# A linear-attention block feeding an erf-gated layer: where one projection piece stands between the chunk products and the end of the previous step's output

## The chip, the cores and the metric

The kernel runs on one core of one Trainium2 chip. The metric is device time in microseconds, the median of several runs. A profile is one execution of its own: it has a time of its own, and a span from its first to its last instruction.

## The reference

Two blocks in a row. The first is a recurrence (RWKV-6) over 768 tokens for 4 batches and 8 heads of 48 values; the second is a dense layer on its output.

```python
# r, k, v, w: (4, 8, 768, 48); u: (8, 48)
for t in range(S):
    cur = einsum('bhd,bhe->bhde', u * k[t], v[t])
    y[t] = einsum('bhd,bhde->bhe', r[t], state + cur)
    state = w[t][..., None] * state + einsum('bhd,bhe->bhde', k[t], v[t])
x = y.transpose(0, 2, 1, 3).reshape(3072, 384)
h = x @ w_in                        # (3072, 2048)
g = h * erf(softplus(h))
out = g @ w_out                     # (3072, 384)
```

All arithmetic is in fp32.

## The kernel before

The tokens are cut into chunks of 128 in two halves of 64. A step handles one chunk of two batches, so there are twelve steps, 0 to 11 (`n_steps`); steps five to eleven go through `attend_late`. Within a half, the products of r and k are made level by level over blocks of doubling width. In the late steps the small levels come from other engines, and TensorE makes levels five and six (`level_products`, L671: 48 rows against 48 or 32 columns). `take_level` (L681) puts the products of level five into the tile `own`, and `scale` (L364) multiplies r and k by the decays of the level, both on VectorE.

The output y of a step is gathered in a PSUM tile in these parts:

- `from_own(s, own, 1)`, the first half of the chunk's own part, 16 matmuls (32 records, L703);
- `fence()`, a small VectorE copy (L712) that reads y, and that the second half waits for;
- `from_own(s, own, 0)`, the second half, 32 records of L703;
- `through_state`, the part from the state, 64 records of L729, for the tiles `s` and `middle`. Behind it ScalarE copies y to `y3` (L737) and to `xT` (L758), and six small transfers on SP's queue (L764) complete `xT`, the input of the dense layer.

A late step finishes the y of the step before it: `before` is s - 1 when that is a late step too, and so is set in steps six to eleven. Between these parts stand pieces of the dense layer of earlier steps, so that TensorE always has something to do. They are named by letters in lists written out by hand, one for each place in the step (`USUAL`, and `LATE` for steps five and eleven); `run_late` carries them out:

- `P`, a piece of the projection of step s - 3 (`project_fast`, L1275: eight matmuls of 128 rows by 128 columns against 192, 16 records); the projection of two chunks takes seven pieces, the second into another PSUM tile, the fourth into what the first has left;
- `H`, a piece of the hidden layer of step s - 1 (`hidden`, L1153, 12 records), which reads `xT`;
- `s`, `ex`, `m`: softplus (L1109) and erf (L1113) on ScalarE, and the product with them on VectorE (L1118);
- `F`, the next stage of `prepare(s + 1)`: decays and small levels of the next step, on GpSimd and VectorE (its first GpSimd instruction, L486, refills the `own` tile of step s - 1).

The place "front" holds `s P` in all late steps. The order of instructions on each engine is the order in which the program issues them; all engines wait for each other by semaphores. The PSUM tiles `m` of the dense layer have two buffers; the tiles `own` and the inputs `in` have two as well, so the input of step s + 1 is loaded (`load_step`, L231) once `through_state` has read that of step s - 1.

Of the kernel before, what the change touches and what calls it, by code (L numbers as in the profile page):

```python
# [17 lines left out]
P = 128  # L18
# [73 lines left out]
def kernel(  # L92
# [71 lines left out]
    def products(shape, n=None):  # L164

        if n is None:
            n = turns["next"]
            turns["next"] = 1 - n
        names = "abc"[: len(shape) - 1]
        return banks[n][:].rearrange(  # L170
            f"p ({' '.join(names)}) -> p {' '.join(names)}", **dict(zip(names, shape[1:]))
        )
# [5 lines left out]
    def load_halves(dst, src):  # L178

        for i in range(2):  # L180
            nc.sync.dma_start(out=dst[:, i], in_=src[:, i])

    def load_w(s):
        ws[s] = ins.tile([P, JP, C], FP32, name="w")
        nc.sync.dma_start(out=ws[s][:], in_=rkw[s][:, 2])
# [34 lines left out]
    def load_v(s):  # L220

        vt = loaded[s][1]
        nc.sync.dma_start(out=vt[:], in_=v[s])

    def load_step(s):
        t = ins.tile([P, 2, JP, C], FP32, name="in")
        vt = ins.tile([P, NH, D], FP32, name="v")
        if s < DIRECT:
            load_halves(t, rkw[s])
        else:  # L230
            nc.sync.dma_start(out=t[:], in_=rkw[s][:, 0:2])  # L231
        if s == DIRECT:
            load_w(s)
        loaded[s] = t, vt
        if s > 3:
            load_v(s)
# [105 lines left out]
    def at(e, p):  # L342

        return rows(e ^ p & 1)
# [298 lines left out]
    def parts_of(s):  # L643

        c, i = divmod(s, SPC)
        in_t, vt = loaded[s]
        made, tots, tot = ready[s]
        ends = tot.rearrange("p (n h) -> p n h", h=NC)
        return c, in_t, vt, made, states[i][c % 2], states[i][1 - c % 2], ends

    def by_pair(t):

        return lambda x, n: t[:, x, n]
# [5 lines left out]
    def level_products(pp, rk, level, ns=range(NJ * NP)):  # L659

        half = 1 << (level - 1)
        m = HC - half if 1 < level <= MASKED else HC if level == 1 else half
        for n in ns:
            for s0 in range(0, C, HC):
                for e in range(NE):
                    right = rk(0, n)[rows(e), s0 : s0 + HC]
                    to = pp[s0 : s0 + m, e, n, :]
                    if level > 1:
                        right = rights(right, half)
                        to = to[:, : HC // 2].rearrange("p (b h) -> p b h", h=half)  # L670
                    nc.tensor.matmul(  # L671
                        to, lhsT=rk(1, n)[rows(e), s0 : s0 + m], rhs=right,
                        start=True,
                        stop=True,
                    )
# [18 lines left out]
    def from_own(s, own, swap):  # L694
        vt = loaded[s][1]
        for j in range(NJ):
            for q in range(0, NP, 2):
                for h in range(NC):
                    e = h ^ swap
                    for p in (q, q + 1):  # L700
                        n = j * NP + p
                        t = slice(h * HC, (h + 1) * HC)
                        nc.tensor.matmul(  # L703
                            y[at(e, p), e, p // 2, j, t],
                            lhsT=vt[t, n * NE + e, :], rhs=own[t, e * JP + n, :],
                            start=swap == 1 and not j and not q, stop=True,
                            skip_group_check=True,
                        )

    def fence():  # L710

        nc.vector.tensor_copy(  # L712
            out=seen[:].rearrange("p (e g t) -> p e g t", e=NE, g=NP),
            in_=y[:].rearrange("p e q j t -> p e (q j) t")[..., HC - 1 : HC + 1],
        )
# [96 lines left out]
    def attend_late(s, run):  # L812

        c, in_t, vt, own, S, S_next, ends = parts_of(s)
        RK = by_pair(in_t)
        before = s - 1 if s - 1 > DIRECT else None
        if before:
            from_own(before, ready[before][0], 1)
            fence()
        pp = products([P, NE, JP, HC], 0)  # L820
        level_products(pp, RK, LOG - 1)
        scale(s, LOG - 1)
        take_level(own, pp, LOG - 1)
        run("front", None)
        if before:
            from_own(before, ready[before][0], 0)
            through_state(before, xTs[before])
            if s + 1 < n_steps:
                load_step(s + 1)
        following = prepare(s + 1) if s + 1 < n_steps else iter(())  # L830
        next(following, None)
        nc.gpsimd.tensor_mul(faded[0][:], S[:], ends[:, :, 0:1].to_broadcast([P, JP, D]))
        next(following, None)
        run("near", None)
        next(following, None)
        kT = kTs[s]
        nc.vector.tensor_mul(
            kT[:].rearrange("p (e n) d -> p n e d", e=NE),
            kT[:].rearrange("p (e n) d -> p n e d", e=NE), spread[s][:],
        )  # L840
        run(0, following)

        pp = products([P, NE, JP, HC], 0)
        level_products(pp, RK, LOG)
        if s + 1 < n_steps:
            spread_blocks(s + 1, pp)
        take_level(own, pp, LOG)
        if s > DIRECT + 1:
            scale(s, LOG)
        run(1, following)  # L850
        if s == DIRECT + 1:
            scale(s, LOG)
        ps = products([P, NC, JP, HC], 0)
        ps = [[ps[:, h]] * NE for h in range(NC)]
        state_part(s, kT, ps)
        run(2, following)
        nc.vector.tensor_add(middle[both], faded[0][both], ps[0][0][both, :, :D])
        run(3, following)
        if s < n_steps - SPC:
            nc.gpsimd.tensor_mul(  # L860
                faded[1][:], middle[:], ends[:, :, 1:2].to_broadcast([P, JP, D])
            )
            nc.vector.tensor_add(S_next[both], faded[1][both], ps[1][0][both, :, :D])
        run(4, following)
# [243 lines left out]
    def softplus_chunk():  # L1108
        nc.scalar.activation(sp_room, chunks[0], AF.Softplus)  # L1109
# [6 lines left out]
    def multiply_chunk():  # L1116
        h, at = started.pop(0)
        nc.vector.tensor_mul(h, h, at)  # L1118
# [304 lines left out]
    def advance(count=None):  # L1423

        while later and count != 0:
            stage, last = later.pop(0)
            stage()
            count = count and count - 1
            if last and not count:
                break  # L1430
# [44 lines left out]
    def run_late(s, tokens, following=None):  # L1475

        for what in tokens.split():
            if what == "A":
                advance()
            elif what == "P":  # L1480
                piece(projs, s - 3)
            elif what == "H":
                piece(hids, s - 1)
            elif what == "F":
                next(following, None)
            elif what == "Q":
                piece(projs, s - 2)
            elif what == "J":
                next(turns["joint"])
            elif what == "w":  # L1490
                next(joining)
            elif what in "uvz":
                activate_pair(what)
            elif what == "T":
                turns["joint"] = hidden_of_two()
            elif what == "t":
                next(mixing_tokens)
            elif what == "f":
                turns.pop("fill")()
            elif what == "s":  # L1500
                softplus_chunk()
            elif what[0] == "e":
                erf_chunk(what[1])
            elif what == "m":
                multiply_chunk()
            elif what[0] == "k":
                to_lane(s - 2, what[1:3], what[3])
            else:
                blend(s - 2, *(int(n) for n in what[1:]))
                for name in {"S3": ("11", "22"), "S4": ("12",)}.get(what, ()):  # L1510
                    lanes.pop(name, None)
# [29 lines left out]
    with tc.manual_schedule(  # L1541
# [15 lines left out]
        for s in range(n_steps):  # L1557
# [44 lines left out]
            def run(n, following):  # L1602
                if n == 3 and s < n_steps - 2:
                    load_rows(s + 2)
                if n == 3 and s + 3 < n_steps:
                    load_w(s + 3)
                run_late(s, LATE.get(s, USUAL)[STAGES_LATE.index(n)], following)
# [12 lines left out]
        s = n_steps  # L1620
# [107 lines left out]
```

## Time and profile before

| | us |
|---|---|
| median of 3 runs | 575.22 (575.2 to 575.34) |
| the profiled execution, its own time | 574.36 |
| its span | 572.6 |
| TensorE matmuls busy | 564.2 |
| TensorE weight loads busy | 500.6 |
| projection pieces, L1275, in the chain that ended last | 33% of the span |
| hidden pieces, L1153, in that chain | 32% of the span |

The chain that ended last is followed back from the last instruction, at each step to what released it. TensorE has 89% of it, VectorE 5%, DMA 2%. The groups of instructions that the change touches (line, engine, shapes, count, then busy us and mean ns of one):

| line | what | count | busy us | mean ns |
|---|---|---|---|---|
| L703 | own part of y, 64 x 48 against 64 | 768 | 15.9 | 220 |
| L729 | state part of y, `middle`, 48 x 48 against 64 | 384 | 7.7 | 217 |
| L729 | state part of y, `s` | 320 | 6.4 | 217 |
| L671 | level five, 48 x 48 against 32 | 768 | 10.8 | 206 |
| L1275 | projection, `w_out_sb` by `h`, 128 x 128 against 192 | 320 | 56.2 | 329 |

Small matmuls of four array tiles run beside each other, so that their busy time in a timeline is much less than the sum of their durations.

### The profile page before, as it was taken

To read this page: it belongs to the slowest core of one execution; us is meant where nothing else is said; L and a number is where in the kernel's file an instruction comes from. 1 tells how busy PE (TensorE), PEld (TensorE's weight loads), DVE (VectorE), ACT (ScalarE), POOL (GpSimd) and SP (SyncE) were. 2 spreads that over 40 slices of the span, in tenths; PEclk is the share of its full clock that TensorE was granted. 3 is DMA by queue.
4 is the path that set the end of the run, shared out by engine and by line. 5 is a ranking of instruction groups with operands and counts; after the bars stand their busy time and mean duration, and the time that the engine had idled before them with its cause. 6 is when DMAs were issued, how large, how long until landed. Compare 5 with 4: busy or idle time off the path is not lost.

```text
span 572.6 us, 16719 instructions
## 1 busy us (share of the span) xinstructions
PE 564.2 (99%) x7320; PEld 500.6 (87%) x7320; DVE 452.7 (79%) x506; ACT 358.5 (63%) x495; POOL 246.8 (43%) x265
## 2 busy tenths in 40 slices
PE   8899999999999999999999999999999999999997
PEld 5688887578998998998998998898898899989997
DVE  8774886999899899799699599599599596477730
ACT  3658877645458858747756766766675771489500
POOL 4557380731885884384285185176075000000000
PEclk9999999999999999999999999999999999999999
DMA  7596671440426324245245236234232201000000
GB/s 256 199 297 269 224 224 43 187 158 10 148 64 188 104 63 163 38 158 168 35 145 176 40 121 198 41 112 166 47 112 84 47 9 35 2 2 1 27 29 27
DMA packets 54082, 63.24 MB, mean 110 GB/s; under 512 B 35161, under 2 KB 40569, under 8 KB 52985
## 3 DMA queue, kind: packets, MB, share of 16 engines
q1 hardware_dynamic: 53624, 61.98, 34.4%
q8 instruction: 57, 0.93, 0.7%
q10 hardware_dynamic: 384, 0.20, 0.1%
q14 instruction: 17, 0.13, 0.1%
HBM read 52.39 MB, written 8.69 MB: 107 GB/s over the span
## 4 chain that ended last, share of the span: by engine, by line
PE 89%; DVE 5%; DMA 2%; ACT 1%; POOL 1%; issue 1%; SPq 0%; DVEq 0%; ACTq 0%; POOLq 0%
PE m L1275 33%; PE m L1153 32%; PE c L1378 6%; PE pp L671 5%; PE m L1185 4%; PE y L703 2%; PE y L729 2%; PE pp L778 2%; DVE in L364 1%; DMA words<-in_moe_w_in 1%; PE pp L990 1%; PE pp L1063 1%; DMA u_sb<-in_u 1%; DVE h L1118 1%; POOL tot_sb L386 0%
## 5 line engine op out<-in xcount | busy, mean ns | idle before, releaser
L1153 PE MATMUL m<-xT,w_in_sb 128*128 128x256 f32 x960 | 214.9, 382 | 0.2 <-ACT h L1162 0.2
L1153 PEld LDWEIGHTS m<-xT,w_in_sb 128*128 128x128 f32 x960 | 179.9, 190 | 25.5 <-ACT h L1162 0.6
L364 DVE TENSOR_TENSOR in<-in,tot_sb 128x1024 f32<-128x1024 f32 (+1 forms) x55 | 77.4, 1408 | 5.9 <-PE pp L671 3.4
L1162 ACT COPY h<-m 128x512 f32<-128x512 f32 x80 | 46.3, 580 | 47.8 <-PE m L1153 47.5
L1275 PE MATMUL m<-mixed,h 128*128 128x192 f32 x320 | 56.7, 331 | 0.0
L1275 PE MATMUL m<-w_out_sb,h 128*128 128x192 f32 x320 | 56.2, 329 | 0.0
L1275 PEld LDWEIGHTS m<-mixed,h 128*128 128x128 f32 x320 | 51.8, 190 | 0.9
L1275 PEld LDWEIGHTS m<-w_out_sb,h 128*128 128x128 f32 x320 | 52.0, 190 | 0.5
L1275 PE MATMUL m<-w_out_sb,room 128*128 128x192 f32 x288 | 49.7, 326 | 0.0
L1275 PEld LDWEIGHTS m<-w_out_sb,room 128*128 128x128 f32 x288 | 47.3, 190 | 0.1
L1113 ACT ACT_TABLE_LOAD x28 | 35.9, 1283 | 10.5 <-DVE h L1118 8.4
L534 POOL TENSOR_TENSOR words<-words 128x384 f32<-128x384 f32 x28 | 39.7, 1448 | 0.0
L671 PEld LDWEIGHTS pp<-in 48*48 48x48 f32 (+4 forms) x2368 | 30.1, 120 | 10.9 <-issue 5.8
L493 POOL TENSOR_TENSOR words<-words,own 128x384 f32<-128x384 f32 x21 | 30.1, 1433 | 22.0 <-DVE words L524 13.0
L1109 ACT ACT_TABLE_LOAD x28 | 35.9, 1283 | 1.8 <-issue 1.3
L486 POOL TENSOR_TENSOR own<-rest 128x384 f32<-128x384 f32 x7 | 9.7, 1384 | 61.0 <-ACT o L1281 61.0
L671 PE MATMUL pp<-in 48*48 48x32 f32 (+4 forms) x2368 | 34.0, 206 | 0.3 <-DVE in L364 0.3
L534 POOL TENSOR_TENSOR rk<-words 128x384 f32<-128x384 f32 x28 | 33.4, 1225 | 0.0
L559 DVE TENSOR_REDUCE sums<-rk 128x16 f32<-128x768 f32 (+2 forms) x31 | 31.6, 1021 | 0.0
L438 POOL TENSOR_TENSOR tot_sb<-tot_sb 128x256 f32<-128x256 f32 (+4 forms) x50 | 29.9, 598 | 3.8
L1109 ACT ACTIVATE room<-h 128x1024 f32<-128x1024 f32 x28 | 29.6, 1057 | 0.3
L319 POOL TENSOR_TENSOR w_out_sb<-w_out_sb,rest 128x768 int32<-128x768 int32 x8 | 18.3, 2290 | 21.9 <-DVE w_out_sb L311 21.9
(214 smaller groups left out, 1008.7 us busy)
## 6 DMA issues: line engine op xcount, KB each, us to landing
in<-in_rkw SPq DMA_DIRECT2D x8, 1024.0 KB, 5.3
words<-in_moe_w_in SPq DMA_DIRECT2D x16, 384.0 KB, 6.3
words<-in_moe_w_out SPq DMA_DIRECT2D x16, 384.0 KB, 4.4
words<-in_rk_rows SPq DMA_DIRECT2D x8, 768.0 KB, 6.4
w<-in_rkw SPq DMA_DIRECT2D x11, 512.0 KB
v<-in_v SPq DMA_DIRECT2D x12, 384.0 KB, 5.7
out<-o SPq DMA_DIRECT2D x23, 192.0 KB, 3.0
in<-in_rkw SPq DMA_DIRECT2D x7, 512.0 KB, 5.9
```

What stands on the lines that cost most here:

```text
L364: nc.vector.tensor_mul(halves, halves, view(tots[level - 1], 0, [[1, n], [2, nb], [0, half]]))
L438: nc.gpsimd.tensor_mul(new, pair[:, :, 0], pair[:, :, 1])
L493: engine.tensor_mul(to, to, of[:, :, None, :].to_broadcast([P, NEAR // 2 // half, half, D]))
L534: engine.tensor_mul(to[:, i], r[:, half:], k[:, part * rows + i, None].to_broadcast([P, half, D]),)
L559: nc.vector.tensor_reduce(out=to, in_=of, axis=mybir.AxisListType.X, op=ALU.add)
L671: nc.tensor.matmul(to, lhsT=rk(1, n)[rows(e), s0 : s0 + m], rhs=right, start=True, stop=True,)
L1109: nc.scalar.activation(sp_room, chunks[0], AF.Softplus)
L1113: nc.scalar.activation(at, sp_room, AF.Erf)
L1153: nc.tensor.matmul(ps[:, ff, :], lhsT=w_in_sb[:, g * FG + f + ff, kk * P : (kk + 1) * P], rhs=xT[:, kk, :], start=kk == 0, stop=kk == KT - 1,)
L1162: nc.scalar.copy(h[:, f : f + FT, :], ps[:])
L1275: nc.tensor.matmul(to, lhsT=a[:, f], rhs=b[:, f], start=start and f == 0, stop=f == FG - 1, skip_group_check=True,)
L1378: nc.tensor.matmul(to[:, f], lhsT=turns["weights"][b][:, i * FT + f], rhs=turns["tokens"][a], start=a + b in STARTS and not f, stop=True, ...
```

## The change

In steps six to eleven, the list of the place "front" is split. Softplus stays where it was, directly behind `take_level`. The projection piece moves behind the second half of y from the chunk, the part through the state, and the load of the next step's input. Step five, which has no step before it of its kind, keeps the whole list.

```diff
         take_level(own, pp, LOG - 1)
-        run("front", None)
         if before:
+            run_late(s, "s")
             from_own(before, ready[before][0], 0)
             through_state(before, xTs[before])
             if s + 1 < n_steps:
                 load_step(s + 1)
+            run_late(s, "P")
+        else:
+            run("front", None)
         following = prepare(s + 1) if s + 1 < n_steps else iter(())
```

On TensorE this gives, for each of the six steps: level five (L671), L703, L729, piece one, piece two, where it was level five, piece one, L703, L729, piece two. On ScalarE the copy behind piece one (L1281) comes after the copies of y (L737, L758). On SP's queue and on VectorE and GpSimd the order of the instructions stays.

## The prediction

> **What bounds the kernel now.** I read the page first, then the busy time by step, then TensorE's and the vector engine's timelines across one step. The page says which engine to price by. Columns: busy us, share of the span, instructions.
>
> ```profile
> PE 564.2 (99%) x7320; PEld 500.6 (87%) x7320; DVE 452.7 (79%) x506; ACT 358.5 (63%) x495; POOL 246.8 (43%) x265
> ```
>
> A busy matmul row may still hide waits, so the stage itself is needed. This row is one late step, from its level-five products to those of the next step (window, length, then busy us of TensorE's matmuls, its weight loads, VectorE, ScalarE, GpSimd, granted clock, DMA share, GB/s).
>
> ```profile
> 366.07:410.37 44.30, 44.30 (x547) 40.60 (x540) 37.41 (x38) 29.24 (x38) 22.93 (x26) 1.00 0.35 105
> ```
>
> TensorE has work in flight for all of the 44.30 us at full clock. The three steps ahead of it are 44.30 us each too. Asked for TensorE's waits between 277 and 490 us, the trace names none. So the end moves only by what TensorE itself spends, or by a new wait on it. Its timeline around the edit (start, busy us, what):
>
> ```profile
> 366.07 0.89 PE L671 MATMUL pp<-in 48*48 48x32 f32 x64
> 366.89 2.87 PE L1275 MATMUL m<-w_out_sb,h 128*128 128x192 f32 x16
> 369.69 0.67 PE L703 MATMUL y<-own,v 64*48 64x64 f32 x32
> 370.17 0.63 PE L729 MATMUL y<-in,s 48*48 48x64 f32 x32
> 370.62 0.63 PE L729 MATMUL y<-in,middle 48*48 48x64 f32 x32
> 371.18 2.87 PE L1275 MATMUL m<-mixed,h 128*128 128x192 f32 x16
> 373.88 2.76 PE L1275 MATMUL m<-w_out_sb,room 128*128 128x192 f32 x16
> 376.48 2.76 PE L1275 MATMUL m<-mixed,room 128*128 128x192 f32 x16
> ```
>
> Read start to start, since the busy times overlap. A projection piece costs 2.60 between two others (373.88 to 376.48), 2.70 behind small matmuls (371.18 to 373.88), and 2.80 with small ones on both sides (366.89 to 369.69). A piece set between two small groups thus pays 0.20 that one in a row of pieces does not, and small groups pay as well where a piece follows: 0.45 for the 32 matmuls from 370.17 to 370.62, but 0.56 for the next 32, ahead of a piece. The step is now small, piece, small, piece; the change makes it small, small, piece, piece.
>
> **The change part by part.** No instruction is added or removed; in each of steps six to eleven the first projection piece (L1275, 16 records) moves behind 32 records of L703 and 64 of L729.
>
> TensorE, start to start, before: 0.82 (L671), 2.80 (piece one), 0.48 (L703), 0.45 and 0.56 (L729), 2.70 (piece two), 2.60 (piece three), in all 10.41. After:
> - L671 no longer ends on a piece. Its 64 records are busy for 0.89, of which the last takes 0.21 (median of that line), so the last starts at 0.68; the next small one follows one spacing later (0.68 over 15 intervals of four is 0.045, of which the four's own starts use some), say 0.71. Gain 0.11, the same as the 0.56 less 0.45 of L729.
> - L703 no longer follows a piece: 0.45 as L729 has, not 0.48. Gain 0.03.
> - L729 still ends on a piece: 0.45 and 0.56 as before.
> - Piece one now follows small ones and is followed by a piece: 2.70, not 2.80. Piece two lies between pieces: 2.60, not 2.70. Gain 0.20.
>
> That is 0.34 a step, 10.07 for 10.41, and for six steps 2.04 us. All of it lies on the engine that has no slack, so it counts in full.
>
> The one seam that the step of before does not contain is L671 followed by L703. Two rows bound it. Level one in step one is followed by state products (64 rows by 48 columns, the shape of L703), and level six by L791; weight loads show it best.
>
> ```profile
> 31.06 1.00 PEld L671 LDWEIGHTS pp<-in 48*62 48x62 f32 x64 [0.33 <-DVE own L1034]
> 31.97 0.81 PEld L778 LDWEIGHTS pp<-v,kT 64*48 64x48 f32 x32
> ...
> 381.77 0.65 PEld L671 LDWEIGHTS pp<-in 48*32 48x32 f32 x64 [0.23 <-issue]
> 382.46 0.20 PEld L791 LDWEIGHTS pp<-ident,over_blocks 48*64 48x64 f32 x4
> ```
>
> In the first pair L778's first load starts at 31.97, before L671's loads end (32.06): no seam. In the second there is a hole of 0.04 (382.42 to 382.46), as ahead of a piece, and the seam costs the 0.11 that a piece costs. I take the first pair: level five's weights are 48 columns wide, like L703's, and those of level six 32. If the second held, L671 keeps 0.82 and L703 its 0.48: gain 0.20 a step, 1.2 us in all.
>
> [...]
>
> [...]
>
> **Waits.** L703 waits on VectorE for the fence (L712, which reads y), and now does so 2.80 sooner.
>
> ```profile
> 366.32 0.17 DVE L712 COPY seen<-y 128x16 f32<-128x16 f32 x1 [3.50 <-PE y L703]
> 367.03 1.23 DVE L364 TENSOR_TENSOR in<-in,tot_sb 128x1024 f32<-128x1024 f32 x1 [0.54 <-PE pp L671]
> 368.18 0.71 DVE L681 COPY_PREDICATED own<-mask_sb,pp 128x512 f32<-128x512 int32 x1
> ```
>
> The fence ends at 366.49 (VectorE idle for 3.50 before it); L703 would start at 366.07 + 0.71 = 366.78, its load some 0.05 ahead. With a hand-over from VectorE to a waiting TensorE of about 0.05 (0.07 is seen the other way, L703's end at 366.25 to the fence at 366.32) the slack is about 0.2. Level five's products are its cover; without them each late 0.1 us costs 0.6 over six steps. In step six VectorE has been idle for 1.86 and in the others for 3.5, so the cover holds. Cost nothing.
>
> Edits that cost nothing, with their cover. ScalarE: softplus (367.59 to 368.65) ends before the state products would (about 368.2 plus 0.2), so the copies of y run near 368.7 instead of 371.31; the piece's copy to o (L1281, 0.32) falls behind them, when the piece ends near 371.1, and then the load for erf (372.53 now) at about 371.4. Nothing on ScalarE is later. Piece four, which writes over what L1281 reads, comes two pieces (5.2) behind piece one. SP: the six xT transfers and the next step's input come 2.7 earlier, and xT is wanted at 388.97 by L1153. GpSimd: L486, which refills the own tile that L703 has read, starts at 370.52 now and may start near 367.9; VectorE's L518 waits 0.43 for what follows from it. VectorE is earlier, not later, for TensorE's later needs (the kT product, the sums that free m). In the last part TensorE's wait for the scalar copy at 540.63 (0.3) moves along.
>
> So 2.04 off 574.36, the profiled execution's own time (span 572.6), is 572.3; the median of the runs shown is 575.22, 0.86 above, and the same saving gives 573.2.
>
> **Rivals.**
> 1. The seam drains (the 382.46 pair). For it: a real row of the same line. Against: other tile width. 575.22 - 1.2 = 574.0.
> [...]
> 3. Slower: L703's wait covers more of VectorE than the fence. In the trace of before L703 starts at 369.69, behind the end of both L364 (368.26) and L681 (368.89), so the trace can't exclude that it waits for take_level. If so TensorE stands from 366.78 to about 368.94, 2.16 a step, less 0.34, times six: 575.22 + 10.9 = 586. Against: in the built program the count waited for is that of the fence, one below that of the scale. It turns a gain to a loss from a wait of 0.34 a step on.
> 4. The time is given back: a later wait on TensorE appears, most likely where H's second m buffer waits for VectorE's sum (ends 389.25, wanted at 388.97 + 1.31 = 390.28, slack 1.0). The shift of 0.34 leaves 0.7. It would give 575.2.
>
> **How the numbers follow.** Forecast 0.80; rival one 0.06; two 0.05; three 0.04; four 0.05. About 0.2% (1.15 us) is what a measurement can tell from no change. Faster: forecast and rival one, 0.86. Same: two and four, 0.10. Slower: three, 0.04. Forecast alone, with 0.30 to 0.38 a step: 572.9 to 573.4. The range adds the seam's other bound (574.0) and 0.1 for the spread of the runs: 572.8 to 574.1.
>
> **What would show it.** In the trace after: a step of 43.96 instead of 44.30; L671 to L703 0.71 start to start, no idle ahead of L703's loads; piece one 2.70 and piece two 2.60; L712 still 0.25 behind L671's start. Wrong would be an idle time of TensorE with VectorE as its releaser at L703, a hole of 0.04 or more in the loads at that seam, or steps still 44.30 long.

## The result, and the profile after

The kernel after takes 577.97 us (median of 16 runs, 575.58 to 583.04), the kernel before 574.68 beside it (16 runs, 572.63 to 579.56). The ratio is 1.0058, with an interval of 1.0033 to 1.0084: slower by some 3.3 us. The forecast of 573.2 was wrong in sign, and its range (to 574.1) does not reach the result. Of the 16 runs after, six have a mean granted clock of 0.994 to 0.997 and take 578.28 to 583.04, ten have 0.999 or 1.0 and take 575.58 to 578.45. The profiled execution took 576.16 (span 574.3), where that of before took 574.36 (572.6).

The page still has TensorE's matmuls (PE) busy for nearly the whole span; before, they were busy for 564.2 us, 99%:

```profile
PE 563.3 (98%) x7320; PEld 500.8 (87%) x7320; DVE 454.5 (79%) x506; ACT 359.0 (63%) x495; POOL 246.4 (43%) x265
```

The steps say more. These are steps seven to eleven of the kernel after, from the level-five products of one step to those of the next (step eleven to the start of its L778), with the columns of the prediction's row:

```profile
276.01:319.98 43.97, 43.97 (x547) 40.53 (x540) 37.53 (x38) 29.25 (x38) 23.45 (x26) 1.00 0.40 118
319.98:364.23 44.25, 44.23 (x546) 40.50 (x540) 37.53 (x38) 29.32 (x38) 23.45 (x26) 1.00 0.40 117
364.23:409.62 45.39, 44.28 (x547) 40.69 (x540) 37.06 (x38) 29.51 (x38) 22.57 (x26) 1.00 0.36 103
409.62:455.31 45.69, 44.27 (x516) 40.69 (x509) 36.95 (x37) 29.48 (x38) 18.31 (x16) 1.00 0.27 76
455.31:478.21 22.90, 21.75 (x350) 21.03 (x340) 19.24 (x27) 13.41 (x19) 0.00 (x0) 1.00 0.05 15
```

Step seven is 43.97 long, and so is step six: the 43.96 that was forecast, 0.33 less than the 44.30 of every step before. Step eight has 44.25, nine 45.39, ten 45.69, and the part of step eleven 22.90 where it had 21.79. The six differences are -0.33, -0.33, -0.05, +1.09, +1.39 and +1.11, in all +2.88. (The unchanged program ahead of step six took 1.13 less in this one execution, so the spans differ by only 1.7.) So two steps gained what was said, one hardly gained and three lost, although the edit is the same in all six. TensorE's timeline of step seven:

```profile
276.01 0.89 PE L671 MATMUL pp<-in 48*48 48x32 f32 x64
276.72 0.64 PE L703 MATMUL y<-own,v 64*48 64x64 f32 x32
277.18 0.63 PE L729 MATMUL y<-in,s 48*48 48x64 f32 x32
277.63 0.63 PE L729 MATMUL y<-in,middle 48*48 48x64 f32 x32
278.19 2.87 PE L1278 MATMUL m<-w_out_sb,h 128*128 128x192 f32 x16
280.89 2.76 PE L1278 MATMUL m<-mixed,h 128*128 128x192 f32 x16
```

L1278 is L1275 of before. And of step nine:

```profile
364.23 0.89 PE L671 MATMUL pp<-in 48*48 48x32 f32 x64
364.94 0.64 PE L703 MATMUL y<-own,v 64*48 64x64 f32 x32
365.40 0.63 PE L729 MATMUL y<-in,s 48*48 48x64 f32 x32
365.85 0.50 PE L729 MATMUL y<-in,middle 48*48 48x64 f32 x18
367.46 0.43 PE L729 MATMUL y<-in,middle 48*48 48x64 f32 x14 [1.11 <-issue]
```

The first three rows stand as in step seven. Then TensorE stops in the middle of 32 matmuls of one line, between the 18th and the 19th, for 1.11 us, and no semaphore ends that: "issue" means that it waited for nothing that the profile shows. In step ten the stop lies between two products with `s` (412.83, 1.42), in step eleven behind the fourth with `middle` (458.35, 1.15). Among TensorE's waits in the whole trace after, these three come first; that of before has none at this line:

```profile
PE y L729 <- issue: 3.7, 3, 1.4
```

(us in total, times, the longest). The chain that ended last holds the three stops as pieces called "issue", 1.11, 1.42 and 1.15 us long.

**Counting the instructions.** Take all of TensorE's records in order of time: matmuls, weight loads, and 90 others, nearly all of them for semaphores. The number of records ahead of each of the three stops leaves the same remainder, 193, on division by 256; such a place in the count is called a border here. (Without the 90 others the remainders differ.) A small stop in step eight (0.34 from one start to the next, inside the moved piece, whose row lasts 3.15 there) does so too. The page's DMA section has a queue of instructions whose size fits TensorE's, the same in both kernels (packets, MB, share):

```profile
q8 instruction: 57, 0.93, 0.7%
```

0.93 MB over 57 packets are 16,384 bytes each, and some 14,700 records of TensorE over 57 are 256 and a bit: one packet brings 256 instructions. (The run below with 1,536 more instructions, six blocks, has 63 packets there.) Cut to the window from 364.4 to 367.6, the DMA view of the kernel after holds one packet and nothing else:

```profile
GB/s 0 0 0 0 0 0 0 205 0 0 0 0 0 0 0 0 0 0 0 0 0 0 0 0 0 0 0 0 0 0 0 0 0 0 0 0 0 0 0 0
...
q8 instruction: 1, 0.02, 2.0%
```

The slices are 0.08 us wide, and the eighth holds the packet's start: 365.03. 2.0% of 16 engines' 3.2 us is 1.02 us. So the border of 256 was passed at 364.40 (behind the 18th matmul of L671), the packet started 0.63 later, was in at 366.03, and TensorE went on 1.43 after that, at 367.46: 3.06 us for a block of 256. The rows of step seven show how fast the small matmuls pass such a block when they are not held: the 46 others of L671 in 0.54, L703 in 0.46, 32 of L729 in 0.45 and 18 in 0.25, about 1.7 us. The theory (F) is that TensorE runs out of instructions.

Before, the piece between level five and L703 lay inside this block: border at 366.24, packet from 367.12 to 368.48, next border at 370.62, that is 4.38 us, and 2.14 from the packet's end to the border, against the 1.43 of the stop in step nine. The piece, 2.80 us, has 32 of the 256 instructions; without it the block reaches 16 products (0.23) further into L729. 4.38 less 2.80, less the 0.14 of the two seams, and 0.23 more are 1.7 again; 3.06 less 1.7 is the stop of step nine (1.32 from start to start).

In steps six and seven the border falls at the end of L671 or behind it (233.05, 276.69), so that the next 256 instructions reach into the projection pieces: 6.6 us for the block of step seven, and no stop. Where a border falls inside L671 or just ahead of it (320.40, 364.40, 409.52, 455.32), the row that follows waited for its rest: 0.34 from one start to the next in step eight, then 1.11, 1.42 and 1.15. In step eight it falls latest, behind about 42 of the 64, so that the next border lies ten records into the moved piece, and the stop is small.

### The profile page after: what moved, and what is told of

The parts are those of the page before. It is cut to its first block, busy times and chain, and to the rows that moved or that the text cites. A ratio compares the mean times of both kernels' runs of the same rounds, so it can differ in the third digit from the quotient of the medians.

```text
span 574.3 us, 16725 instructions
## 1 busy us (share of the span) xinstructions
PE 563.3 (98%) x7320; PEld 500.8 (87%) x7320; DVE 454.5 (79%) x506; ACT 359.0 (63%) x495; POOL 246.4 (43%) x265
## 4 chain that ended last, share of the span: by engine, by line
PE 82%; DVE 8%; issue 4%; POOL 2%; DMA 2%; ACT 1%; SPq 0%; DVEq 0%; POOLq 0%; ACTq 0%
PE m L1278 33%; PE m L1156 29%; PE c L1381 6%; PE pp L671 5%; DVE in L364 2%; PE m L1188 2%; PE y L703 2%; PE y L729 2%; PE pp L778 1%; DMA words<-in_moe_w_in 1%; PE pp L993 1%; DMA u_sb<-in_u 1%; DVE own L681 1%; POOL w_out_sb L1219 1%; DVE h L1121 1%
## 5 line engine op out<-in xcount | busy, mean ns | idle before, releaser
L1278 PE MATMUL m<-w_out_sb,h 128*128 128x192 f32 x320 | 56.4, 330 | 0.0
L1278 PE MATMUL m<-mixed,h 128*128 128x192 f32 x320 | 56.1, 329 | 0.0
L1278 PEld LDWEIGHTS m<-w_out_sb,h 128*128 128x128 f32 x320 | 51.9, 190 | 1.0 <-issue 0.3
L1278 PEld LDWEIGHTS m<-mixed,h 128*128 128x128 f32 x320 | 52.1, 190 | 0.4
L1278 PE MATMUL m<-w_out_sb,room 128*128 128x192 f32 x288 | 49.7, 326 | 0.0
L1278 PEld LDWEIGHTS m<-w_out_sb,room 128*128 128x128 f32 x288 | 47.3, 190 | 0.1
L671 PEld LDWEIGHTS pp<-in 48*48 48x48 f32 (+4 forms) x2368 | 30.1, 120 | 11.2 <-issue 6.0
L671 PE MATMUL pp<-in 48*48 48x32 f32 (+4 forms) x2368 | 34.0, 206 | 0.4 <-DVE in L364 0.4
```

Of the source, the lines that this page charges most:

```text
L671: nc.tensor.matmul(to, lhsT=rk(1, n)[rows(e), s0 : s0 + m], rhs=right, start=True, stop=True,)
L1278: nc.tensor.matmul(to, lhsT=a[:, f], rhs=b[:, f], start=start and f == 0, stop=f == FG - 1, skip_group_check=True,)
```

## The experiments

The rivals to theory F were that the load of the next step's input, which now starts ahead of the piece, gets in the way (L), and that the stop is tied to the order or the place of the instructions rather than to their count.

**The load put back behind the piece.** The kernel after, with

```diff
             through_state(before, xTs[before])
+            run_late(s, "P")
             if s + 1 < n_steps:
                 load_step(s + 1)
-            run_late(s, "P")
```

> The change, with the load of the next step's input put back behind the projection piece (all transfers of the load then start where they did before). Theory F (TensorE runs out of instructions: they come in blocks of 256, and the small matmuls pass a block in under 2 us, faster than the next block comes): nothing changes on TensorE, its holes in the state products of steps 9, 10 and 11 stay at 1.1 to 1.4 us each, at the same instructions, and the time stays about 3 us above before (577 to 578.5). Rival L (the 1 MB load, started earlier, gets in the way of what TensorE reads or fetches): the holes are gone, steps 43.97 long, 2 us below before.

Measured: 578.92, ratio 1.007 (1.0044 to 1.0097). Steps six to ten 43.97, 43.97, 44.60, 45.68, 45.65. The stops are at the same instructions:

```profile
371.82 0.43 PE L729 MATMUL y<-in,middle 48*48 48x64 f32 x14 [1.40 <-issue]
```

Again the 19th product with `middle` of step nine. With the load back in its old place the stops are no shorter, so L falls. (The start of this program is that of the kernel after, and yet its trace has one more stop there, of 1.92 at 20.24 and also at remainder 193, behind a packet that started 3.4 after its border: one trace of a kernel doesn't show all that the next may have.)

**128 more instructions in step five,** in the kernel after and in the kernel before: the products of level five are made twice there, which gives the same values.

```diff
         level_products(pp, RK, LOG - 1)
+        if s == DIRECT + 1:
+            level_products(pp, RK, LOG - 1)
```

> The change, with the level-five products of step five made twice, which puts 128 more instructions (64 matmul records, 64 weight loads) on TensorE ahead of step six and some 0.75 us. Nothing else moves. Theory F: the borders of the 256-instruction blocks shift by half a block against the steps, so the holes leave steps 9, 10, 11 and appear in steps 6, 7 and 8, some 1.3 to 1.6 us each; steps 9, 10, 11 become 43.9 to 44.0 long. Rivals L and W (a wait on data that is late in the late steps): the holes stay in 9, 10, 11.

Measured: 578.14, ratio 1.0056 (1.0029 to 1.0083). The steps six, seven and nine of it:

```profile
234.35:279.74 45.39, 44.21 (x547) 40.63 (x540) 37.07 (x38) 29.51 (x38) 22.57 (x26) 1.00 0.38 114
279.74:325.36 45.62, 44.19 (x547) 40.60 (x540) 37.52 (x38) 29.51 (x38) 22.45 (x26) 1.00 0.38 114
...
369.33:413.30 43.97, 43.97 (x547) 40.53 (x540) 37.53 (x38) 29.25 (x38) 23.43 (x26) 1.00 0.37 106
```

The loss has changed places: steps six and seven have it now, nine to eleven are free. Nothing in those steps was edited against the kernel after; only the count of instructions ahead of them is another (and the start of step six, 2.3 us later). Both stops are at remainder 193 again. One part missed: step eight was to have a stop and has none. There the border lay at 324.99, in L703 ahead of L671; TensorE was still in the slow hidden pieces when the next packet started, at 322.28, 2.7 before the border. The block then passed in 1.62 us without a stop, which is the free pace of the row of small matmuls.

> The kernel before with the same doubled products in step five. Theory F: the piece between the small groups keeps every block above 4.3 us, so no hole appears at any phase of the blocks: steps six to ten stay 44.30 long, and the time is before plus 0.75. If holes of over 0.3 us appeared here, the phase would matter without the change as well, and the change alone would not be what makes them.

Measured: 574.89, ratio 0.9997 (0.9976 to 1.0018), all late steps 44.30 and no stop. This shift of the phase (where the borders fall in a step) does nothing by itself while the piece is in its old place.

**The change in steps six and seven alone.**

```diff
         if before:
-            run_late(s, "s")
+            late = s in (6, 7)
+            run_late(s, "s" if late else "s P")
 ...
-            run_late(s, "P")
+            if late:
+                run_late(s, "P")
```

> The change in steps six and seven alone; steps eight to eleven as before. Theory F: no block border pair falls inside the small matmuls of these two steps, so both are 43.97 long and all others 44.30, no hole anywhere, the time 0.7 below before (ratio 0.9988). Rivals L and W, by which any step that has the change can get a hole: 43.97 or a hole of about 1 us, not the same in each run.

Measured: 573.56, ratio 0.998 (0.996 to 1.0). Steps 43.97, 43.97, 44.30, 44.30, 44.29, and TensorE has no wait of any kind in the late steps.

**The piece between L703 and L729,** in all six steps. L703 is as early as in the kernel after, and the row of small matmuls is cut behind it.

```diff
             run_late(s, "s")
             from_own(before, ready[before][0], 0)
+            run_late(s, "P")
             through_state(before, xTs[before])
             if s + 1 < n_steps:
                 load_step(s + 1)
-            run_late(s, "P")
```

> Half of the change in steps six to eleven: the second half of y from the chunk directly behind level five, then the projection piece, then the part through the state. As many seams between small matmuls and pieces as before, so nothing is saved; the longest run of small matmuls is 256 instructions (first half, level five, second half) instead of 384. Theory F: a block of 256 takes at least the 2.8 us of the piece, or is asked for before the run begins, so there is no hole, every step is 44.30 long, and the time is that of before. Rival W (the state products stop for data of their own): the holes stay in steps 9 to 11.

Measured: 573.49, ratio 0.9982 (0.9962 to 1.0001), all steps 44.31, no stop. So it is not the early L703 that costs; the piece covers the supply in this place as in its old one. There is also no gain in the steps, because this order has as many seams as that of before.

**Only small matmuls for six blocks.** The kernel before, with the level-five products of step five made thirteen times, 1,536 more instructions.

```diff
+        if s == DIRECT + 1:
+            for _ in range(12):
+                level_products(pp, RK, LOG - 1)
```

> The kernel before with the level-five products of step five made thirteen times: 1536 more instructions in a row, which are six whole blocks, so that the phase of later steps stays. It prices the supply by itself. The array alone would take 12 times 0.71, 8.5 us. Theory F: each block of 256 waits for its own transfer, 3.0 to 3.8 us from border to border, so six blocks take 18 to 23 us, with a hole at every border and all later steps at 44.30. Rivals L and W: 8.5 us, no hole.

Measured: 600.78, one run; step five 69.82 instead of 43.12. Its timeline:

```profile
193.38 2.79 PE L671 MATMUL pp<-in 48*48 48x32 f32 x128 [1.82 <-issue]
197.38 2.79 PE L671 MATMUL pp<-in 48*48 48x32 f32 x128 [1.21 <-issue]
203.30 2.78 PE L671 MATMUL pp<-in 48*48 48x32 f32 x128 [3.14 <-issue]
```

Each row is 128 matmuls with their 128 weight loads, one block, and a stop lies on either side of each. From border to border it takes 3.45 to 4.00 us, once 5.92, where the packet started only at 201.09, 3.7 behind the border, beside other transfers of up to 441 GB/s. That supply is a limit is shown; the sum was missed, 26.7 where 18 to 23 were expected (the bare matmuls were to cost 8.5). One reason is that packet, the other stands in the busy time by stretch, with the granted clock in the third column from the end:

```profile
193.38:197.38 4.00, 2.79 (x128) 2.65 (x128) 0.00 (x0) 2.34 (x2) 0.14 (x1) 0.50 0.24 51
215.00:222.00 7.00, 7.00 (x47) 6.94 (x44) 6.46 (x9) 1.28 (x2) 1.64 (x1) 0.62 0.01 2
```

From 193.01, within the first of the stops, the clock is granted at half: a row of 128 takes 2.79, where the 142 ahead of that stop, at the full clock, took 1.78. The work behind the rows pays for it too, with 0.62 over 7 us.

**Half of the piece ahead, half behind.** The kernel before; piece one is cut behind its fourth product, and the second half moves behind `through_state`.

```diff
             from_own(before, ready[before][0], 0)
             through_state(before, xTs[before])
             if s + 1 < n_steps:
                 load_step(s + 1)
+            run_late(s, "P")
```

```diff
-        product(m0[:, lo], a11, b11, True)
+        for f in range(FG):
+            nc.tensor.matmul(
+                m0[:, lo], lhsT=a11[:, f], rhs=b11[:, f], start=f == 0, stop=f == FG - 1,
+                ...
+            )
+            if f == FG // 2 - 1 and 3 <= s <= 8:
+                yield
```

> The kernel before with the first projection piece of steps six to eleven cut in two: four matmuls stay ahead of the second half of y (1.5 us of cover instead of 2.8), four go behind the state products. Seams cost what they did (5.50 for pieces one and two), so steps without a hole are 44.30. Theory F: the block that holds the run takes about 3.2 us unhindered in steps 9 to 11, and the next block comes 3.0 to 3.8 us after the border: holes of 0 to 0.6 us there, none in steps 6 and 7. A cover that only mattered by being there or not would give no hole at all.

Measured: 574.52, ratio 1.0026 (1.0003 to 1.0048). Steps eight to ten:

```profile
321.35:365.64 44.29, 44.29 (x546) 40.59 (x540) 38.13 (x38) 29.35 (x38) 23.28 (x26) 1.00 0.40 117
365.64:410.32 44.68, 44.60 (x547) 40.76 (x540) 38.14 (x38) 29.36 (x38) 23.27 (x26) 1.00 0.36 104
410.32:454.69 44.37, 44.37 (x516) 40.67 (x508) 37.66 (x37) 29.36 (x38) 19.13 (x16) 1.00 0.28 78
```

Half a piece is 1.50 us of cover. The blocks of steps nine to eleven last 3.54, 3.18 and 3.15, with a stop of 0.29 in step nine and next to nothing in ten and eleven. The length of the cover counted here: 1.7 of free pace and 1.5 of piece come to 3.2, about what the supply took in these steps of the kernel after (3.0 to 3.3).

**Steps eight to eleven alone, with the phase set at the program's start:** 33 small matmuls take the place of one warm-up matmul, 128 instructions more by count.

```diff
-        stay_warm(6)
+        stay_warm(5)
+        pass_by(33)
```

> Made from theory F: the change in steps eight to eleven alone, with the blocks shifted by half a block from the start (one of the six warm-up matmuls at the start gives way to 33 small ones, 128 instructions more). Steps 6 and 7 keep the old order, since after the shift their run would hold a border pair. Theory F: steps 8 to 11 are 43.97 long, 6 and 7 44.30, no hole, the time 1.3 below before (573.0) if the start is as long as before. Rivals: holes in steps 9 to 11 as in the full change, 4 us above that.

Measured: 578.21, ratio 1.008 (1.005 to 1.0111). The late steps came as expected, 44.30, 44.30, 43.97, 43.97, 43.96, without a stop. The start did not: level five of step six begins at 237.69 instead of 233.17. The early part has small matmuls too, and the new phase put borders among them while the weights were being loaded:

```profile
22.78 0.48 PE L1004 MATMUL pp<-s,ident 128*128 128x384 f32 x1 [2.16 <-issue]
39.97 0.35 PE L671 MATMUL pp<-in 48*60 48x32 f32 x10 [1.18 <-issue]
```

The packets of these two blocks started 3.0 and 3.8 us after their borders (17.41 and 33.76). The two stops, 3.3 in all, fit theory F: a shift can be paid for wherever else the count decides. How much of the 4.5 is the shift's is not shown, since in the first 50 us of the traces of before and after six packets start 3.0 to 4.0 behind their borders, and the unshifted start had a stop too in the run with the load behind the piece.

**All six steps, with the phase set behind step seven.** The kernel after, with the level-six products of step seven made twice: 128 more instructions in a group of small ones far from the edit. Beside it the version with steps six and seven alone was timed again.

```diff
         level_products(pp, RK, LOG)
+        if s == DIRECT + 3:
+            level_products(pp, RK, LOG)
```

> The kernel after, with the products of level six of step seven made twice: 128 more small TensorE instructions in a group that already has small ones, far from the edit, so no new seam. Theory F (TensorE runs out of instructions in the long row of small matmuls where a border of 256 falls just ahead of it): steps six and seven keep their phase and are free of holes, steps eight to eleven take the phase of the kernel with 128 more in step five, which is free in these steps. Steps 43.97, 43.97 plus the doubled group's 0.65 to 0.7, then 43.97, 43.97, 43.97, 43.96 and a last part of about 21.5. Over the six steps about 1.3 less than before; time 572.9 to 573.6 where before has 574.3, ratio 0.997 to 0.9985. If the loss came from the order itself (transfers, later waits, whatever is not tied to the count of instructions), steps eight to eleven stay at 44.25 to 45.7 and the kernel is slower than before by 0.7% as the kernel after is.

Measured: 572.66, ratio 0.9973 (0.9955 to 0.9992), before 574.58. Steps seven to ten:

```profile
276.08:320.58 44.50, 44.50 (x610) 41.06 (x604) 37.55 (x38) 29.38 (x38) 23.44 (x26) 1.00 0.41 117
320.58:364.55 43.97, 43.97 (x547) 40.53 (x540) 37.52 (x38) 29.24 (x38) 23.40 (x26) 1.00 0.40 118
364.55:408.52 43.97, 43.97 (x547) 40.53 (x540) 37.54 (x38) 29.23 (x38) 23.43 (x26) 1.00 0.37 106
408.52:452.48 43.96, 43.96 (x516) 40.52 (x508) 37.08 (x37) 29.24 (x38) 19.29 (x16) 1.00 0.28 79
```

The 64 useless matmuls cost 0.53 in step seven, and all six steps have the 0.33: 220.37 from step six to step eleven instead of 221.49, and 0.34 less in step eleven. It adds work to the kernel after and is faster than that of before.

> The change in steps six and seven alone, timed again beside the other, since its interval just reached 1. Steps 43.97, 43.97, then 44.30; no holes in late steps; 0.66 less than before in the late steps, ratio 0.998 to 0.9995.

Measured: 573.56, ratio 0.9983 (0.9966 to 1.0), steps 43.97, 43.97, 44.30, 44.30, 44.29 and no late stop. The gain of 0.66 that its trace shows lies at the edge of what this measurement can tell: the piece between L703 and L729 had 0.9982 too, with no step shorter than before. It is the steps in the traces that carry the gain, here and with all six steps.

## Why the prediction was wrong, point by point

- **The seams** were right. L671 to L703 takes 0.71 (forecast 0.71), L703 to L729 0.46 (0.45), piece one 2.70, piece two 2.60, the step 43.97 (43.96). Rival one, the drain, did not come.
- **The load of L703** is not held. In step nine its first load starts at 364.91, while the last of L671's loads end at 365.01 and its last product, 0.21 long, has just started. The chance of rival two, 0.05 for 574.4, was that of a load held until that product is out, which no run shows.
- **The fence** costs nothing, as said: TensorE has no wait on VectorE at L703 in any step. Rival three falls, and with it the mechanism on which the whole chance of "slower" stood.
- **No later wait** took the gain back: where no instruction is missing, as in the last version, the steps are 43.97 long (44.50 with the added products) and TensorE waits for nothing in them. Rival four falls.
- **The step that failed** is "edits that cost nothing, with their cover". The moved piece was priced as 16 records with two seams, and as cover for the fence. It was also the cover under which the next 256 instructions came in: 2.80 us in a block that without it passes in 1.7 and takes 3.0 to 3.3 to supply in these steps. The statement that no instruction is added or removed was true, and beside the point: what counted here is how many instructions follow each other without slow work among them. Now level five, L703 and L729, with the 64 instructions of L703 ahead of them, are 384 in a row.
- **The trace of before could have told it.** The prediction rests on the waits between 277 and 490 us, where TensorE has none. In the list for the whole span, which was on hand, TensorE's second wait is one without a releaser, in the weight part of the start:

```profile
PE pp L671 <- issue: 0.8, 1, 0.8
```

  It is a stop in the middle of 32 equal matmuls at 27.88, also at remainder 193; its packet ran from 25.62 to 26.51, and TensorE went on 1.38 later. In steps nine to eleven of the same trace the packets start 0.88, 0.94 and 0.89 behind their borders and take 1.36, 1.24 and 0.95. With 1.38 taken for each as the time to go on, the three blocks take 10.4 to supply, and without the piece they pass in three times 1.7: 5.3 lost, less six times 0.34, is slower by some 3.3. That sum is made with hindsight; the traces have 2.9, with other packet times and a little lost in step eight, the medians 3.3.
- **The chance** of slower, 0.04, was that of one mechanism, the fence. Cover was counted on the engines and queues that the edit touches by name; the engine's own supply of instructions was not among them.

Left open: why some packets start late (3.0 to 4.0 us behind the border for three in the first 50 us of the trace of before and three in that of after, between which and their borders 273 to 408 GB/s were moved; not isolated), and how much of the spread of the runs comes from them, since each kernel has one trace. What lowered the clock to 0.994 to 0.997 in six of the runs after was not shown either.

## What to carry to other kernels

Before slow work is moved out of a row of small instructions, count the instructions that will then follow each other, and compare the time in which they pass with the time in which the engine's instruction queue brings them; here 256 small ones pass in 1.6 to 1.7 us and come in 3.0 to 4.0 (5.9 once). A stop with "issue" as its releaser in the middle of equal instructions, at equal remainders of the count, was the sign here, and what took it away was slow work within the row (573.49, no late stop) or a shift of the count (572.66), which is to be tried over the whole program (a shift at its start gave 578.21). Read the waits of the whole span, also where the stage in question has none.

## What the runs showed of the hardware

- TensorE's instructions came in packets of 16,384 bytes, 256 instructions each (57 packets for some 14,700 records, before and after). In the late steps of these two traces the next packet starts 0.60 to 1.42 us behind 24 of the 32 borders that lie in small matmuls, and takes 0.89 to 1.45 us. Where TensorE stopped for it, it went on 1.38 to 1.45 us after its end (1.43, 1.42 and 1.43 in the three stops after, 1.45 in the small one of step eight, 1.38 in the stop at 27.88 before).
- In the rows of small matmuls and their weight loads the supply was not hidden: a block of them took 1.62 us without a stop (step eight of the run with 128 more instructions in step five), about half of the 3.06 that a block took where TensorE stopped for it (step nine after). The block of step seven after, which reaches into the projection pieces, took 6.6 us and had no stop.
- In the step with the 1.62 TensorE came to the border out of slow work, and the packet was under way 2.7 us before it.
- In the run with six blocks of nothing but small matmuls, the granted clock fell to 0.50 within the first stop (1.82 us), stayed there while stops of 0.7 to 3.1 us followed, and was 0.62 over the 7 us behind them. The three stops of 1.1 to 1.4 us of the kernel after, some 45 us apart, left it at 1.0 in their steps.
